# Chunked attention with a gated convolution on one Trainium2 core: a new order of the same pieces, new buffer homes, and a new division of small work between engines

## The chip, the cores and the metric

The kernel runs on one core of a Trainium2 chip (trn2). The metric is the device time of one execution in microseconds (us); the kernel before has three timed runs and one profiled execution. "ns" marks nanoseconds. The engines are TensorE (PE in the rows; PEld are its weight loads), VectorE (DVE), ScalarE (ACT), GpSimd (POOL) and SyncE (SP), whose queue issues the loads and stores.

## What is computed

Inputs q, k, v are float32 of shape (8, 8, 576, 64): batch, heads, sequence, head size. Attention runs inside chunks of 64 positions; its output, with the heads side by side, is x of shape (8, 576, 512):

```python
scores = np.matmul(q_c, k_c.transpose(0, 1, 2, 4, 3)) / 8
attn = np.exp(scores - np.max(scores, axis=-1, keepdims=True))
attn = attn / (np.sum(attn, axis=-1, keepdims=True) + 1e-09)
x = np.matmul(attn, v_c)
gate = 1.0 / (1.0 + np.exp(-sum(conv_w[j] * xp[:, j:j + S, :] for j in range(5))))
out = (gate * (x @ w_val)) @ w_out
```

xp is x with four rows of zeros ahead of each batch (a causal convolution of five taps per column). w_val and w_out are 512 x 512.

## The kernel before, in words

The 4608 rows of x are cut into 9 groups g of 512. A group has two head pairs p and, for the matrix products, four column blocks of 128 (m, c, hp) and four row blocks t. All work is cut into small pieces, and one long string, ORDER (line 18), lists 1157 of them; a loop (line 516) reads the string and calls a function for each, and every engine does its own pieces in the order of the list. Nothing reorders them: a late piece holds up all that stands behind it on its engine. A second table, SLOTS (line 95), says which of a few fixed buffers each tile takes, in order of creation. A piece that writes a buffer waits until the readers of what it held are done. The large matrix products work on float32 split in two rounded parts (high and low), three matmuls for each product.

The pieces, with their engine where no letter is added (D at the end of a name puts a piece on VectorE, G on GpSimd):

- Loads on SyncE: lq, lk, lv (g, p), 512 KB each, into six buffers ld0 to ld5; lw n c, a 512 KB block of w_val (n = v) or w_out (n = o), into one of four acc buffers; lc, the taps. st g t stores 256 KB.
- Weights: w1 to w7, wb, w9 turn a loaded block into its high and low parts (VectorE, ScalarE, GpSimd).
- TensorE: W n, n warm-up matmuls on zeros, whose result nobody reads; S g p b, 32 score matmuls of 64 x 64 (two halves b in one two-bank score buffer); sp, four matmuls that subtract a row maximum; T g p, eight transposes; A g p, 64 matmuls of attention times v, into two of four banks ps; V g m c, three matmuls of 128 x 512 of x @ w_val (lines 448 to 454), four pieces c to a bank; P g t c, three matmuls of the last product (lines 477 to 483).
- Softmax: mx (row maxima, VectorE), sb (subtract, VectorE, reads the score buffer and so frees it), ex and ep (exponential, ScalarE), ea (another form, 16 exponentials with sums, ScalarE), sm (sums and reciprocals, VectorE), ng and rc (small, VectorE), nm (divide, GpSimd), ec (transposed scores out of their banks, ScalarE).
- x: xr (high part) and xc (copy) on ScalarE, xd (low part) on VectorE, each on a half u; all three read the bank. hl fills the halo (GpSimd).
- Convolution: k0 (first tap, ScalarE), k g hp j (taps 1 to 4, VectorE, one multiply-and-add of 128 x 516 each), sg (sigmoid, ScalarE; exponential and sigmoid need different tables, and a change loads one).
- Gate: vc (x @ w_val out of its bank, ScalarE), gs (times the gate, VectorE) or gm (both in one, VectorE), gr (high part, ScalarE), gd (low part, GpSimd). oc copies a finished output block (ScalarE).

```python
    def pr(g, t, c):
        ...
        for n, (y, w) in enumerate(((gh, wh), (gh, wl), (gl, wh))):
            run(E.matmul, o_ps[g, t], lhsT=y[g, c][:, ts], rhs=w["o"][:, c, :], start=(c == 0 and n == 0),
                stop=(c == NH - 1 and n == 2))
```

So P g t c needs gr g c and gd g c, and, for c = 0 or the first of a bank's four, the bank; V g m c needs xr and xd of both halves.

Of the kernel before, what the change touches and what calls it, by code (L numbers as in the profile page):

```python
# [21 lines left out]
lv 1 0,sb 1 0,xc 0 0 1,xr 0 0 1,wb v 0,T 0 1,xd 0 0 0,ex 1 0,xd 0 0 1,S 1 1 0,w1G v 3,ec 0 1,S 1 1 1,sm 1 0,w7G v 1,
V 0 3 0,lq 2 1,w5 v 3,lw o 0,w2 v 3,mx 1 1,A 0 1,lk 2 1,nm 1 0,xc 0 0 0,lw o 1,lw o 3,V 0 2 0,sb 1 1,xr 0 1 0,lk 3 0,
w6 v 1,T 1 0,xr 0 1 1,w3 v 3,wbD v 1,xc 0 1 0,S 2 0 0,xc 0 1 1,w4 v 3,S 2 0 1,w6 v 2,xd 0 1 0,w7G v 3,ec 1 0,V 0 3 1,
lq 4 0,xd 0 1 1,lq 3 0,V 0 2 1,w3 c 0,w1 c 0,wb v 2,mx 2 0,w6 v 3,A 1 0,w5 c 0,w2 c 0,ex 1 1,w4 c 0,wb v 3,sb 2 0,
V 0 2 2,lv 1 1,w5 o 0,V 0 3 2,xr 1 0 0,w3 o 0,w9,V 0 2 3,sm 1 1,ex 2 0,k0G 0 1,V 0 3 3,hl 1,vc 0 2,w1G o 0,S 2 1 0,
# [10 lines left out]
V 2 1 0,w4 o 1,sg 0 1,V 2 0 3,k 1 2 1,w6 o 3,k0 2 0,V 2 1 1,gdD 0 0,vc 2 0,w7 o 1,V 2 3 2,gr 0 3,k 1 0 2,V 2 1 2,
k0 1 1,k 1 2 2,V 2 2 0,gr 0 2,gdD 0 3,w6 o 1,V 2 1 3,w3 o 2,w2 o 2,ng 4 0,P 0 1 0,gs 0 1,vc 2 1,k 1 2 3,V 2 2 1,gr 0 1,
wbD o 1,V 2 3 3,gdD 0 1,V 2 2 2,w4 o 2,ex 3 1,P 0 2 0,k 1 3 1,V 2 2 3,vc 2 3,w7 o 2,T 3 0,gdD 0 2,w6 o 2,sm 3 1,vc 2 2,
P 0 1 1,wb o 2,ea 4 0,P 0 3 0,wbD o 3,P 0 0 0,k 1 1 1,P 0 0 1,nmD 3 1,P 0 1 2,P 0 1 3,k 1 3 2,P 0 0 2,k 1 1 2,P 0 0 3,  # L40
ec 3 0,k 1 0 3,P 0 2 1,k 1 1 3,oc 0 1,P 0 3 1,k 1 0 4,k0 2 1,P 0 2 2,oc 0 0,k0D 2 2,k 1 1 4,T 3 1,k 2 2 1,P 0 3 2,
k 1 3 3,sg 1 0,A 3 0,k 1 2 4,ec 3 1,rc 4 0,P 0 2 3,sg 1 1,k 1 3 4,lk 5 0,xr 3 0 0,P 0 3 3,k 2 1 1,hl 3,oc 0 2,k 2 0 1,
S 4 1 0,nm 4 0,oc 0 3,S 4 1 1,xd 3 0 0,xr 3 0 1,A 3 1,lq 5 1,xd 3 0 1,xc 3 0 0,lk 5 1,mx 4 1,xc 3 0 1,V 3 3 0,lk 7 1,
gsG 1 0,xr 3 1 0,V 3 2 0,k0 2 3,xd 3 1 0,V 3 2 1,xr 3 1 1,gsG 1 1,xc 3 1 0,xd 3 1 1,V 3 3 1,gr 1 0,k 2 2 2,V 3 1 0,
sg 1 2,gd 1 0,sb 4 1,V 3 3 2,xc 3 1 1,V 3 2 2,k 2 3 1,V 3 0 0,k 2 1 2,V 3 0 1,k 2 3 2,ex 4 1,V 3 2 3,k 2 2 3,V 3 1 1,
k 2 3 3,vc 3 2,V 3 0 2,k 2 1 3,V 3 3 3,k 2 1 4,sg 1 3,P 1 0 0,k 2 3 4,gr 1 1,V 3 1 2,k 2 0 2,V 3 1 3,gdD 1 1,k 2 0 3,
T 4 0,vc 3 1,k 2 2 4,P 1 0 1,gs 1 2,sg 2 2,V 3 0 3,k 2 0 4,ec 4 0,gsG 2 2,P 1 1 0,sm 4 1,gr 1 2,S 5 0 0,vc 3 3,S 5 0 1,
hl 4,sg 2 1,gdD 1 2,nm 4 1,P 1 1 1,lv 7 1,vc 3 0,mx 5 0,st 0 2,P 1 3 0,gr 2 2,lq 6 0,sg 2 3,P 1 3 1,sb 5 0,sg 2 0,
P 1 2 0,k0 3 1,gs 2 0,P 1 0 2,k0 3 3,gs 1 3,S 5 1 0,k 3 1 1,gr 1 3,S 5 1 1,k0 3 2,gdD 2 2,P 1 1 2,gd 1 3,lv 4 0,st 0 1,
gr 2 0,mx 5 1,P 1 2 1,lk 6 1,P 1 3 2,k 3 1 2,gd 2 0,P 1 2 2,sb 5 1,ex 5 0,P 1 0 3,k0 3 0,gs 2 1,P 1 3 3,gs 2 3,gr 2 1,  # L50
P 1 1 3,sm 5 0,gd 2 1,P 1 2 3,oc 1 1,oc 1 0,S 6 0 0,k 3 1 3,oc 1 2,S 6 0 1,st 1 0,ex 5 1,A 4 0,k 3 3 1,lv 4 1,lk 8 1,
# [5 lines left out]
V 4 3 3,hl 5,sg 3 1,gsG 3 2,V 4 2 0,oc 2 3,V 4 1 0,vc 4 3,gs 3 1,nm 5 0,gr 3 2,V 4 1 1,sm 6 0,sg 3 0,A 5 1,k 4 1 3,
V 4 2 1,nm 6 0,xr 5 1 0,lv 5 0,st 0 0,xr 5 1 1,T 5 0,xd 5 1 0,sg 3 3,sb 6 1,V 4 2 2,xc 5 1 0,xc 5 1 1,V 4 2 3,gsG 3 3,
ec 5 0,xd 5 1 1,S 7 0 0,S 7 0 1,gs 3 0,gr 3 1,A 5 0,k 4 3 1,vc 4 2,lq 7 1,gr 3 0,k0D 5 2,V 4 0 0,mx 7 0,xr 5 0 0,
gd 3 0,xc 5 0 1,V 4 1 2,xc 5 0 0,k0D 5 3,V 4 0 1,k 4 1 4,k0 5 1,V 4 1 3,k 4 3 2,gr 3 3,V 4 0 2,xr 5 0 1,xd 5 0 0,  # L60
gd 3 3,V 4 0 3,xd 5 0 1,P 3 3 0,gdD 3 1,gd 3 2,vc 4 0,vc 4 1,P 3 2 0,k0 5 0,P 3 3 1,k 4 3 3,sg 4 1,V 5 0 0,k0 4 2,
# [5 lines left out]
xd 6 0 1,S 7 1 0,S 7 1 1,gs 4 1,A 6 1,lv 7 0,k 5 0 4,st 3 1,mx 7 1,lq 8 0,T 7 0,xc 6 1 1,lv 8 1,xc 6 0 1,st 3 0,
V 5 2 2,k 5 3 4,xr 6 1 0,V 5 1 0,gs 4 3,xr 6 1 1,xd 6 1 0,V 5 2 3,sg 5 3,xcD 6 1 0,sg 4 0,V 5 1 1,k 5 1 4,gr 4 1,
k0G 6 3,V 6 1 0,vc 5 2,xd 6 1 1,V 6 1 1,sb 7 1,gsG 4 0,V 6 0 0,V 6 2 0,gdD 4 1,k0G 6 2,V 6 2 1,k0D 6 0,gsG 5 3,V 6 2 2,
ex 7 1,V 6 1 2,gr 4 3,k 6 2 1,gsG 4 2,V 6 1 3,gr 4 0,ecD 7 0,V 6 2 3,k0 6 1,V 6 0 1,k 5 2 4,gr 4 2,V 6 0 2,sm 7 1,  # L70
vc 6 1,hl 7,gd 4 0,V 5 1 2,vcD 6 2,S 8 1 0,nm 7 1,sg 5 2,S 8 1 1,A 7 0,sg 5 1,lk 8 0,st 2 3,gdD 4 2,lv 8 0,V 6 0 3,
# [500 lines left out]
```

## Time and profile before

| | us |
|---|---|
| median of 3 timed runs | 285.98 (285.41 to 287.75) |
| span of the profiled execution, first to last instruction | 286.4 |
| TensorE busy | 274.4 (96%) |
| VectorE busy | 245.8 (86%) |
| ScalarE busy | 198.1 (69%) |
| GpSimd busy | 105.2 (37%) |

Times in rows count from the first instruction. Every instruction of the list comes from one helper, so all rows carry line 160; they are told apart by tile names (buffer numbers left out: ps for ps3; t is t2 and t4 with a digit, t2i one buffer of t2). A "busy" TensorE includes matmuls that overlap: a 128 x 512 matmul lasts about 400 ns, but the next starts 0.23 us after it.

### The profile page before, as it was taken

What the parts mean: (1) busy time and instruction counts of PE and PEld (TensorE: products, weight loads), DVE (VectorE), ACT (ScalarE), POOL (GpSimd) and SP (SyncE); (2) the same over time, 40 slices, a digit from 0 to 9 for tenths busy, and PEclk for the clock granted to TensorE, in tenths of its full rate; (3) what the DMA queues carried; (4) which work ended last, traced back from release to release, by engine and by line L of the source; (5) the groups of instructions that cost most, each with busy time, mean ns of one, the idle gap of its engine ahead of it and who ended that gap; (6) DMA issues with size and microseconds to landing.
All of it is one profiled execution on the core that took longest, in us unless ns stands there. A gap on an engine that the chain in (4) does not pass through costs nothing.

```text
span 286.4 us, 7971 instructions
## 1 busy us (share of the span) xinstructions
PE 274.4 (96%) x3344; PEld 217.3 (76%) x3347; DVE 245.8 (86%) x357; ACT 198.1 (69%) x451; POOL 105.2 (37%) x93
## 2 busy tenths in 40 slices
...
GB/s 280 416 391 359 380 239 130 169 181 260 3 2 78 222 0 185 221 223 211 86 185 2 73 201 218 173 144 44 39 0 1 39 89 61 0 100 49 110 171 195
DMA packets 14291, 42.47 MB, mean 148 GB/s; under 512 B 1712, under 2 KB 1712, under 8 KB 14256
## 3 DMA queue, kind: packets, MB, share of 16 engines
...
## 4 chain that ended last, share of the span: by engine, by line
PE 69%; DVE 19%; DMA 3%; issue 3%; POOL 2%; ACT 2%; SPq 0%; POOLq 0%
PE ps L160 61%; DVE acc L160 8%; PE s L160 5%; DVE t L160 4%; PE et L160 4%; DVE rs L160 3%; DMA ld<-in_v 2%; DMA ld<-in_q 1%; POOL acc L160 1%; POOL t L160 1%; DVE mx L160 1%; ACT x L160 1%; DVE t2o L160 1%; DVE t4a L160 0%; DVE x L160 0%
## 5 line engine op out<-in xcount | busy, mean ns | idle before, releaser
L160 DVE SCALAR_TENSOR_TENSOR acc<-x,cw,acc 128x516 f32<-128x516 f32 (+1 forms) x144 | 105.1, 771 | 0.9 <-POOL acc L160 0.6
L160 PE MATMUL ps<-t,v_hi 128*128 128x512 f32 x240 | 85.3, 402 | 0.0
L160 PE MATMUL ps<-t,v_lo 128*128 128x512 f32 x136 | 53.9, 396 | 0.0
L160 PEld LDWEIGHTS ps<-t,v_hi 128*128 128x128 f32 x240 | 45.2, 188 | 11.0 <-issue 0.5
L160 PE MATMUL ps<-o_hi,t 128*128 128x512 f32 x120 | 46.4, 403 | 0.8 <-ACT x L160 0.7
L160 PE MATMUL ps<-o_lo,t 128*128 128x512 f32 x76 | 30.0, 395 | 0.0
L160 DVE TENSOR_REDUCE mx<-s 128x16 f32<-128x1024 f32 x18 | 21.8, 1211 | 9.3 <-PE s L160 9.2
L160 PEld LDWEIGHTS ps<-t,v_lo 128*128 128x128 f32 x136 | 25.7, 189 | 5.1
L160 PEld LDWEIGHTS ps<-o_hi,t 128*128 128x128 f32 x120 | 22.5, 188 | 7.3 <-ACT x L160 1.1
L160 POOL TENSOR_TENSOR t<-e_row,rs 128x1024 f32<-128x1024 f32 x13 | 26.4, 2033 | 4.2 <-DVE rs L160 3.4
L160 PEld LDWEIGHTS s<-ld,ld 64*64 64x64 f32 x1152 | 19.4, 139 | 9.6 <-issue 7.7
L160 ACT CAST t<-ps 128x512 fp32r<-128x512 f32 x34 | 19.4, 596 | 10.0 <-PE ps L160 8.1
L160 PE MATMUL s<-ld,ld 64*64 64x64 f32 x1152 | 22.0, 227 | 2.9 <-issue 1.9
L160 ACT ACTIVATE e_row<-s,mx 128x64 f32<-128x64 f32 x64 | 19.0, 352 | 4.7 <-DVE mx L160 4.7
L160 POOL COPY x<-x 128x16 f32<-128x16 f32 x8 | 2.8, 354 | 52.6 <-DVE acc L160 44.9
L160 PEld LDWEIGHTS ps<-t,ld 64*64 64x64 f32 x960 | 16.3, 140 | 5.0 <-issue 2.1
L160 PE MATMUL ps<-t,ld 64*64 64x64 f32 x960 | 18.1, 225 | 1.9 <-DVE t2i L160 1.1
L160 POOL TENSOR_SCALAR acc<-x,cw 128x516 f32<-128x516 f32 (+1 forms) x7 | 12.7, 1820 | 19.2 <-ACT x L160 7.4
L160 ACT ACTIVATE acc<-x,cw 128x516 f32<-128x516 f32 (+1 forms) x24 | 17.6, 740 | 1.9 <-DVE x L160 1.8
L160 ACT ACT_TABLE_LOAD x14 | 18.0, 1283 | 0.9 <-PEq L561 0.7
L160 DVE TENSOR_REDUCE rs<-e_row 128x16 f32<-128x1040 f32 x14 | 17.2, 1228 | 1.6 <-ACT e_row L160 1.6
L160 ACT COPY x<-ps 128x512 f32<-128x512 f32 (+3 forms) x38 | 16.0, 476 | 3.3 <-issue 2.0
...
## 6 DMA issues: line engine op xcount, KB each, us to landing
...
```

Of the source, the lines that this page charges most:

```text
L160: return tc.keep_in_program_order(fn(*args, **kwargs))
```

## The change

The list ORDER is written anew: the same 1157 pieces for the same work, in another order on all engines. SLOTS is new for nearly all buffers. The warm-up matmuls go from 31 (W 8, 15, 6, 2) to 17 (W 10, 4, 1, 2). Some pieces change engine. By kind, before to after: first taps k0 on ScalarE 24 to 20, VectorE 5 to 3, GpSimd 7 to 13; gd on VectorE 21 to 17, GpSimd 15 to 19; gs on VectorE 18 to 17, GpSimd 14 to 15; nm on GpSimd 14 to 13, VectorE 4 to 5; xc on VectorE 9 to 4, ScalarE 27 to 32; oc on VectorE 11 to 10; vc on VectorE 3 to 4; ec on VectorE 2 to 3; w7 on VectorE 2 to 5, GpSimd 6 to 3; w1 on VectorE 1 to 2; wb on VectorE 4 to 3. The rest of the code changes only so that halves of x may come in either order:

```diff
-ORDER = """zw,lk 0 0,zi,lq 0 0,W 8,lw v 2,lw v 0,lq 0 1,zr 1,zm,lk 0 1,lw v 1,zr 0,lv 0 0,lq 1 0,S 0 0 0,S 0 0 1,W 15,mx 0 0,
+ORDER = """zw,zi,zr 0,zr 1,lk 0 0,lq 0 0,W 10,zm,lw v 2,w1 v 2,w3 v 2,w2G v 2,S 0 0 0,S 0 0 1,mx 0 0,sb 0 0,lw v 0,w5 v 0,w5 v 2,
...
-    mx="021021021021021021",
+    mx="001111122000000111",
...
+    def x_of(g):
+        if g not in xs:
+            xs[g] = tile_of("x", [P, NH, XW], F32)
+        return xs[g]
+
     def hl(g, on=G):
 
-        xs[g] = x = tile_of("x", [P, NH, XW], F32)
+        x = x_of(g)
...
     def xr(g, p, u):
-        if u == 0:
+        if (g, p) not in xh:
             xh[g, p] = tile_of("xh", [P, 2, T], F32R)
...
     def xd(g, p, u):
-        if u == 0:
+        if (g, p) not in xl:
             xl[g, p] = tile_of("xl", [P, 2, T], F32R)
```

The first pair of fences is SyncE's list at the start, its 8th to 17th entries before and its 8th to 19th after (ld, acc: the buffers; in_q, in_k, in_v, in_moe_w_val, in_moe_w_out: the inputs). Before:

```order
L160 DMA ld2_102<-in_v 128x1024
L160 DMA ld1_104<-in_q 128x1024
L160 DMA ld5_157<-in_k 128x1024
L160 DMA ld0_161<-in_k 128x1024
L160 DMA acc1_166<-in_moe_w_val 128x1024
L160 DMA ld4_226<-in_q 128x1024
L160 DMA ld3_230<-in_q 128x1024
L160 DMA ld1_334<-in_v 128x1024
L160 DMA ld5_341<-in_k 128x1024
L160 DMA raw_cw_343<-in_moe_conv_w 128x40
```

After:

```order
L160 DMA acc3_193<-in_moe_w_out 128x1024
L160 DMA acc0_210<-in_moe_w_val 128x1024
L160 DMA ld4_234<-in_k 128x1024
L160 DMA ld5_243<-in_q 128x1024
L160 DMA ld0_247<-in_k 128x1024
L160 DMA ld1_289<-in_v 128x1024
L160 DMA ld2_332<-in_q 128x1024
L160 DMA ld3_404<-in_q 128x1024
L160 DMA ld0_406<-in_v 128x1024
L160 DMA ld5_443<-in_v 128x1024
L160 DMA raw_cw_446<-in_moe_conv_w 128x40
L160 DMA ld1_473<-in_q 128x1024
```

The v of group 0 (lv 0 0) was the 8th load and is now the 13th, behind two weight blocks and the q and k of group 1; the 20th entry after, not shown, is lk 2 0.

The second pair is TensorE's list around S 2 0, the scores of group 2 (s: score buffer; et: transpose banks; ps: V banks; t42, t43 and so on: high and low part of x). Before:

```order
L160 MATMUL et0_476<-ident_61,t49_459 128x128 x8
L160 MATMUL s0_490<-ld5_341,ld3_230 64x64 x32
L160 MATMUL ps2_410<-t42_348,v_hi_66 128x512
L160 MATMUL ps2_410<-t42_348,v_lo_68 128x512
L160 MATMUL ps2_410<-t4a_365,v_hi_66 128x512
```

After:

```order
L160 MATMUL ps0_458<-t42_326,v_hi_66 128x512
L160 MATMUL ps0_458<-t42_326,v_lo_68 128x512
L160 MATMUL ps0_458<-t43_340,v_hi_66 128x512
L160 MATMUL s0_482<-ld2_480,ld1_473 64x64 x32
L160 MATMUL et0_517<-ident_61,t48_515 128x128 x8
```

The piece V 0 3 1 (three rows on ps) now stands ahead of the scores of group 2, and the transposes T 1 0 behind them.

The third pair is SyncE's list around the v of group 2, second pair (lv 2 1). Before:

```order
L160 DMA ld2_823<-in_v 128x1024
L160 DMA acc2_825<-in_moe_w_out 128x1024
L160 DMA ld0_1007<-in_v 128x1024
L160 DMA ld5_1015<-in_k 128x1024
L160 DMA ld4_1029<-in_k 128x1024
```

After:

```order
L160 DMA ld0_853<-in_q 128x1024
L160 DMA ld4_897<-in_v 128x1024
L160 DMA ld4_997<-in_v 128x1024
L160 DMA ld0_1006<-in_k 128x1024
L160 DMA ld2_1096<-in_k 128x1024
```

Before, lv 2 1 (ld0_1007) takes the buffer of lq 3 1, which S 3 1 reads; now (ld4_997) it takes that of lv 2 0 (ld4_897), which A 2 0 reads. On TensorE, A 2 0, T 2 1, two V pieces and S 4 0 stood between S 3 1 and A 2 1; now S 3 1, T 2 1 and seven V pieces stand between A 2 0 and A 2 1.

## Rows read from the trace of the kernel before

**Rows 1.** The page: busy us, share of the span, instructions of each engine.

```profile
PE 274.4 (96%) x3344; PEld 217.3 (76%) x3347; DVE 245.8 (86%) x357; ACT 198.1 (69%) x451; POOL 105.2 (37%) x93
```

**Rows 2.** Stretches: length, then busy PE, PEld, DVE, ACT, POOL; clock, DMA share, GB/s.

```profile
10.00:20.00 10.00, 9.09 (x219) 5.98 (x220) 9.11 (x15) 6.24 (x10) 4.06 (x4) 1.00 1.03 410
20.00:30.00 10.00, 7.34 (x189) 5.45 (x192) 9.41 (x15) 9.47 (x16) 7.87 (x7) 1.00 0.99 362
30.00:40.00 10.00, 10.00 (x191) 7.87 (x184) 6.96 (x10) 6.23 (x13) 8.25 (x9) 0.83 0.79 287
...
60.00:70.00 10.00, 9.17 (x184) 7.63 (x177) 9.28 (x13) 9.10 (x20) 7.18 (x6) 1.00 0.87 298
...
180.00:190.00 10.00, 8.99 (x100) 7.10 (x98) 9.33 (x11) 6.59 (x10) 9.25 (x9) 1.00 0.25 95
190.00:200.00 10.00, 9.81 (x216) 8.01 (x219) 9.82 (x13) 9.28 (x18) 6.11 (x5) 1.00 0.38 131
200.00:210.00 10.00, 9.33 (x60) 7.33 (x51) 9.97 (x16) 5.01 (x16) 3.96 (x3) 1.00 0.08 28
```

**Rows 3.** The chain that ended last: start us, us, what.

```profile
27.82 1.94 issue
...
59.46 5.08 DMA ld<-in_v
...
220.13 62.66 PE ps L160 x386
```

**Rows 4.** Stretches around the first hole, columns as in rows 2.

```profile
27.00:30.00 3.00, 1.06 (x41) 0.75 (x43) 2.58 (x6) 2.82 (x5) 1.80 (x2) 1.00 1.02 385
...
31.00:34.50 3.50, 3.50 (x66) 2.61 (x68) 3.50 (x6) 0.87 (x2) 1.75 (x2) 0.51 1.01 359
```

**Rows 5.** Timeline of PE, 118 to 123 us: start us, us, instruction, count.

```profile
118.98 0.40 PE L160 MATMUL ps<-o_hi,t2o 128*128 128x512 f32 x1
119.31 1.16 PE L160 MATMUL s<-ld,ld 64*64 64x64 f32 x64
...
121.33 0.49 PE L160 MATMUL ps<-o_hi,t2q 128*128 128x512 f32 x1
121.67 0.39 PE L160 MATMUL ps<-o_lo,t2q 128*128 128x512 f32 x1
121.89 0.40 PE L160 MATMUL ps<-o_hi,t 128*128 128x512 f32 x1
```

**Rows 6.** Timeline of DVE and POOL, three places where both work in SBUF.

```profile
128.90 2.87 DVE L160 SCALAR_TENSOR_TENSOR acc<-x,cw,acc 128x516 f32<-128x516 f32 x4
128.11 1.71 POOL L160 TENSOR_SCALAR acc<-x,cw 128x516 f32<-128x516 f32 x1 [2.02 <-issue]
139.78 1.80 DVE L160 TENSOR_TENSOR t<-t,t2n 128x512 f32<-128x512 f32 x1 [0.42 <-ACT t2n L160]
139.75 1.29 POOL L160 TENSOR_TENSOR t2p<-t2c,t2d 128x512 f32<-128x512 f32 x1
189.92 2.13 DVE L160 TENSOR_TENSOR t2o<-t,t2n 128x512 fp32r<-128x512 f32 x1
```

**Rows 7.** Groups of instructions: count, busy us, mean ns of one, idle before.

```profile
L160 DVE SCALAR_TENSOR_TENSOR acc<-x,cw,acc 128x516 f32<-128x516 f32 (+1 forms) x144 | 105.1, 771 | 0.9 <-POOL acc L160 0.6
L160 DVE TENSOR_REDUCE mx<-s 128x16 f32<-128x1024 f32 x18 | 21.8, 1211 | 9.3 <-PE s L160 9.2
L160 POOL TENSOR_SCALAR acc<-x,cw 128x516 f32<-128x516 f32 (+1 forms) x7 | 12.7, 1820 | 19.2 <-ACT x L160 7.4 <-DVE x L160 5.1 <-ACT t2n L160 2.9
L160 ACT ACT_TABLE_LOAD x14 | 18.0, 1283 | 0.9 <-PEq L561 0.7
```

**Rows 8.** Timeline of the first loads' users: start us, us, instruction, idle before.

```profile
5.47 1.99 PE L160 MATMUL s<-ld,ld 64*64 64x64 f32 x64 [0.71 <-DMA ld<-in_q]
7.18 0.63 POOL L160 TENSOR_SCALAR t<-acc 128x512 f32<-128x512 f32 x1 [5.79 <-DMA acc<-in_moe_w_val]
```

**Rows 9.** Waits of PE: who waited for whom, us in total, times, longest.

```profile
PE ps L160 <- DVE t2i L160: 1.1, 1, 1.1
```

More of the change, by code (lines that the diff above doesn't have):

```diff
@@ L22 @@
[L22 to L26, printed above, removed]
@@ L37 @@
[L37 to L41, printed above, removed]
@@ L42 @@
[L42 to L51, printed above, removed]
@@ L57 @@
[L57 to L61, printed above, removed]
@@ L67 @@
[L67 to L71, printed above, removed]
@@ new lines @@
+xc 2 1 0,S 4 0 0,S 4 0 1,V 2 3 0,V 2 3 1,xd 2 1 0,gr 0 3,k0 1 2,V 2 2 0,V 2 2 1,mx 4 0,k 1 2 1,ng 4 0,xc 2 1 1,gr 0 1,
+gdD 0 1,V 2 3 2,V 2 1 0,w7 o 2,w4 o 1,k 1 0 3,V 2 3 3,w5 o 1,w7 o 1,hl 2,k 1 2 2,k 1 3 1,ex 3 1,T 3 0,k0 2 2,k 1 2 3,
+w6 o 2,gr 0 0,k0 1 1,V 2 2 2,w6 o 3,gdD 0 0,V 2 0 0,V 2 0 1,V 2 1 1,V 2 0 2,V 2 0 3,k 1 3 2,ec 3 0,gr 0 2,vc 2 3,w6 o 1,
+vc 2 0,V 2 1 2,V 2 1 3,vc 2 1,sm 3 1,gdD 0 2,k0 2 0,k0 2 3,wbD o 2,k 1 1 1,wbD o 3,P 0 1 0,V 2 2 3,k 1 2 4,gdD 0 3,
+P 0 0 0,lk 6 0,wb o 1,P 0 0 1,vc 2 2,P 0 0 2,P 0 1 1,nmD 3 1,lv 3 0,P 0 1 2,P 0 1 3,k 1 3 3,ea 4 0,k 1 1 2,k 2 0 1,
@@ new lines @@
+k 3 1 3,A 4 0,oc 1 1,gdD 2 1,sm 5 1,nmD 5 1,xr 4 0 1,xd 4 0 1,gr 2 0,gdD 2 0,S 6 0 0,S 6 0 1,k0G 3 2,xc 4 0 0,mx 6 0,
+k 3 2 1,T 4 1,gd 2 3,k 3 3 1,gr 2 2,gd 2 2,xr 4 0 0,k 3 2 2,lv 4 1,P 2 2 0,P 2 2 1,P 2 2 2,P 2 2 3,ec 4 1,xd 4 0 0,
+ex 5 0,k 3 3 2,k 3 3 3,xc 4 0 1,oc 2 2,P 2 1 0,P 2 1 1,k 3 0 1,k 3 0 2,lq 6 1,P 2 1 2,P 2 1 3,oc 2 1,sm 5 0,nm 5 0,
+A 4 1,xc 4 1 0,xr 4 1 1,lk 7 0,T 5 1,xr 4 1 0,xc 4 1 1,k0G 4 3,k0G 4 2,ec 5 1,P 2 3 0,P 2 0 0,P 2 0 1,xd 4 1 0,sb 6 0,
+P 2 3 1,ex 6 0,k 3 0 3,k 3 3 4,k 3 2 3,k 3 2 4,P 2 3 2,P 2 3 3,k0G 4 1,P 2 0 2,P 2 0 3,oc 2 0,st 2 0,k 3 0 4,oc 2 3,
```

132 lines of the change are left out of this document (76 added, 56 removed).

## The prediction, made before the changed kernel ran

> **What bounds the kernel now.** I read four views: the busy shares, the same by stretches, the chain of waits, and single instructions by name where the chain changes hands. TensorE is busy 274.4 of 286.4 us and VectorE 245.8 [rows 1]. By stretches [rows 2] there are three parts. Until about 35 us TensorE has holes (7.34 of 10 us from 20 to 30) and VectorE too (6.96 from 30 to 40). Then both run almost without a pause, TensorE with 0.83 us missing at 60 to 70 and 1.01 and 0.67 us at 180 to 190 and 200 to 210. The chain shows the last 62.66 us before the final copy and store as one stretch of TensorE [rows 3], so the end is the time at which TensorE reaches it, and that is its work plus what it lost before.
>
> What was lost early has two pieces. At 27.82 us TensorE stands for 1.94 us in the middle of the scores of group 2; the profile names no releaser ("issue") [rows 3]. It had been busy for 1.06 of those 3 us, and from 31 to 34.5 us its granted clock is 0.51, the 1.2 GHz level [rows 4]. That costs 3.5 x 0.49 = 1.7 us.
>
> In the middle the two engines are locked together. A matmul waits for a difference, a released bank or a scaled row that VectorE makes, and its date is set by the VectorE work that stands ahead in the list. I count both queues up to a place. On TensorE a V or P piece is 0.70 us (three matmuls, 0.23 apart, 121.67 to 121.89 [rows 5]), half a score piece 0.55, a transpose piece 0.87, an A piece 1.03. A VectorE instruction takes its group's mean less the 0.06 by which neighbours overlap (four k in 2.87 us, 0.72 each [rows 6]; means in [rows 7]). Before S 5 1 0 stand 88 V or P, 22 half scores, 9 T, 8 A and the four row-maximum matmuls: 90.7 us. VectorE's queue up to sb 5 0, which frees the bank, holds 146 instructions (48 k, 11 mx, 8 sb, 8 sm, 16 xd, the rest small): 99.7 us. I call 9.0 us the lead that this place asks. The tightest such places before lie at 9 to 9.6 us from 70 us to 165 us, about 8 after that.
>
> **The change, part by part.**
>
> Start. The loads come at 410 GB/s [rows 2], so 512 KB take 1.28 us; the third has landed by 7.18, where GpSimd starts on it [rows 8]. In the new list lk 1 0 is the 12th load, so about 7.1 + 9 x 1.28 = 18.6 us, lv 0 0 the 13th, 19.9, lv 0 1 the 16th, 23.7, lk 2 0 the 19th large one, 27.6 (the first pair of fences in the section on the change). I follow the chain, each step with the mean of its group: S 0 1 waits for the sixth load, about 11.0, and takes 2.0 us, as S 0 0 did at 5.47 behind slow warm-up matmuls and a hole [rows 8]; S 1 0 ends 19.8, A 0 0 21.0, mx 1 0 and sb 1 0 22.3, ex 1 0 23.9, ec 0 1 24.9, A 0 1 25.9; sm 1 0, w4 v 3, mx 1 1, sb 1 1 on VectorE end 29.0 and free the score bank; S 2 0 ends 30.1. Before, S 2 0 ended at 30.57, with T 1 0 done and V 0 3 1 not; now the reverse, 0.87 against 0.70 us. So TensorE stands 0.3 us better there, and its holes are spread: none from 27 us on is over 0.6 us. I expect no fall of the clock after it, 1.7 us, though no row shows how it behaves in the new pattern. Bounds: with a wait like the unnamed one and the low clock again, -0.3 + 1.9 = +1.6; with the chain faster by 1.6 as well, -3.6. I take -2.0, what the chain gives. The 14 warm-up matmuls that go cost nothing by themselves: what follows them waits for a load or for VectorE. VectorE has no hole from 30 to 40 in this chain; it had 3.0 us, so it runs 3.0 us earlier.
>
> The load lv 2 1. Before, it went out at 59.46, when S 3 1 was done, and took 5.08 us, with only A 2 0, T 2 1, two V and S 4 0 (4.4 us) ahead of its use; TensorE stood 0.8 us [rows 2, 3]. Now it waits for A 2 0, and S 3 1, T 2 1 and seven V, 6.9 us, stand between. 5.08 fits: -0.8. It fails from a landing of 6.9 us on; if the queue holds it back so long, 0.
>
> Late waits. 1.01 + 0.19 + 0.67 = 1.9 us of holes from 180 to 210 [rows 2]; the longest, 1.1, is A 7 0 on a bank that VectorE copies out (vcD 6 2, into t2i) [rows 9]. There the old list asks a lead of 166.1 us of TensorE work against 174.2 of VectorE, 8.1, and 8.0 at P 5 0 0 (189.2 against 197.2). The new list asks 5.9 at V 7 0 2 (177.1 against 183.0) and 2.4 at V 8 1 2 (209.6 against 212.0). With 2 to 5 us of slack these go: -1.9, bounds -1.9 and 0.
>
> Changes of shape. Between V or P and 64-wide pieces TensorE loses 0.1 us going in (118.98 to 119.31) and 0.1 coming out (121.33 to 121.67) against 0.23 [rows 5]. Such visits fall from 20 to 18, 0.4 us; T pieces right after V or P fall from 12 to 5, each with the 0.1 on the way out, 0.7 us. Where VectorE sets the pace it is worth nothing, so I take half: -0.5, bounds -1.1 and 0.
>
> The pace in the first half. Here the new list asks more. At V 3 1 0: 64 V or P, 22 half scores, 9 T, 8 A, 73.9 us, against 127 VectorE instructions, 84.5: 10.6. At P 2 2 0: 96, 26, 10, 9, 100.4 us, against 163 instructions up to gdD 2 0 (51 k, 12 mx, 9 sb, 9 sm, 17 xd, 6 gd, 6 gs), 112.0: 11.6. Against the 9.6 that TensorE met before, that is 2.0 more. VectorE is 3.0 us earlier and TensorE 2.0 + 0.8 = 2.8; the difference, 0.2, pays part, and TensorE must wait 1.8. Bounds: 0 (gdD 2 0 could meet a free VectorE) and +3 (VectorE not earlier). I take +1.8.
>
> Loads of the other engines. VectorE's pieces change by -2 first taps, -5 xc, -4 gd, -1 gs, -1 oc, +1 vc, +1 nm, +1 ec, +3 w7, +1 w1, -1 wb, about -4 us; that is in the leads above. ScalarE: -1.2 us of copies and taps, but 16 table loads instead of 14, +2.6 [rows 7]; it is 69% busy [rows 1], so 0, and at most +1. GpSimd takes on six first taps (1.82 each), four gd, one gs, one wb and gives up one nm, three w7, a w1: +12 us on 105. It waits for others two thirds of the time, but it slows VectorE when both read SBUF: at 139.78 a VectorE product of two SBUF tiles took 1.80 us beside a GpSimd one of 1.29, and at 189.92 one took 2.13 [rows 6]; six such long ones from 139 to 200 us, 6.6 us in all, on 105 us of GpSimd. Pro rata +0.8, but no long one before 139 us, where VectorE sets the pace in the new list: +0.2, bounds 0 and +7.
>
> The Trainium skill (SBUF — State Buffer, on the two separate sides) says that a VectorE instruction with two SBUF inputs and a GpSimd one that reads SBUF exclude each other for the whole instruction. At 139.78 the trace agrees. Beside the first tap at 128.11 (1.71 us) it does not: four k with two SBUF inputs ran in 2.87 us, unstretched [rows 6]. By the rule the added 12 us would block VectorE where it holds such work; the second rival below gives what that costs as a mechanism of this kernel.
>
> **Sum.** -2.0 - 0.8 - 1.9 - 0.5 + 1.8 + 0.2 = -3.2 us on the profiled execution: 286.4 to 283.2. What lies behind the last matmul (one copy, one store, 3.6 us) stays [rows 3]: 286.4 - 220.13 - 62.66. The span is 0.4 us above the median 285.98, so 282.8 as a median, 1.1% less. About 1%, 2.9 us, is what a measurement of this kernel can tell from no change.
>
> **Rivals.**
>
> First: the start does not hold. The unnamed wait of 1.94 us comes at another score piece, or the clock falls after the new hole at 23 to 25 us (1.5 us in this chain). For it: the loads stay at 400 GB/s and the new list has the same burst of small matmuls there; against it: the holes are more evenly spread. Start 0 instead of -2.0; VectorE is then no earlier either, so the pace still costs 1.2 (2.0 less the 0.8 of lv 2 1): 285.98 - 0.8 - 1.9 - 0.5 + 1.2 + 0.2 = 284.2; with half of a second such wait 285.2, which I take.
>
> Second, slower: GpSimd holds up VectorE. Each of the six added first taps, four gd and the gs falls between two-input instructions of VectorE and costs the 1.1 us of 139.78: 11 x 1.1 = 12 us, of which the seven before 130 us, where the lead is tight, count whole: +7.7 instead of +0.2. That gives 290.3; from four of them before 130 us on (4.4 us) it outweighs the gains. For it: 139.78 and 189.92; against it: 128.11, and no long one in the first 139 us. With five of the seven, 5.5 us, it is 288.1.
>
> Third: no pace is paid and the start is 1.6 us better still: 282.8 - 1.8 - 1.6 = 279.4. For it: VectorE is 4 us lighter; against: the wait on banks stays a chain through two engines.
>
> Fourth: the list moves much but the lead at P 2 2 0 keeps TensorE at its old date, and the late holes only move: 286.0.
>
> **How the numbers follow.** Forecast 0.50, its own range 281.0 to 284.2, two thirds of it below 283.1, the mark of 1%. First rival 0.18 (no change). Second 0.15 (slower). Third 0.09 (faster). Fourth 0.08, of which 0.02 on the slow side. Faster by over 1%: 0.33 + 0.09 = 0.42. Slower: 0.15 + 0.02 = 0.17. Within 1%: 0.17 + 0.18 + 0.06 = 0.41. The range for 8 in 10 leaves out half of the second rival and most of the third: 280.0 to 288.0.
>
> **What would show it.** Right: no stretch with a granted clock below 1 from 27 to 40 us; VectorE above 9.5 of 10 us from 30 to 40; TensorE's row on in_v gone; no hole over 0.5 us from 180 to 210; small holes at V 3 1 0 and P 2 2 0, 1 to 2 us in all, on VectorE. Wrong: an unnamed wait again before 40 us; k, gs or gd of 1.6 us and more before 130 us; a wait of TensorE on ScalarE longer than 1 us; a chain that after 220 us still runs through VectorE.

## The result, and the profile after

The changed kernel takes 289.91 us (289.79 to 290.64), the kernel before 285.70 in the same comparison: ratio 1.0142, interval 1.0096 to 1.0189. It is slower, by 4.2 us, where 282.8 was forecast. Executions of one kernel scatter by 2 us and more, so the sections below give medians and the ratio to the kernel before with its interval. The ratio leaves out executions of more than 1.5% above the fastest of their kernel, which a median keeps (three of ten at f4_before_cold), so it is not always the quotient of two medians.

The page after, busy times and the granted clock in 40 slices (7.2 us each):

```profile
PE 273.1 (95%) x3333; PEld 218.3 (76%) x3333; DVE 251.6 (87%) x350; ACT 200.5 (69%) x453; POOL 118.3 (41%) x100
PEclk9676999999999999999999999999999999999999
```

The clock is low from the second slice to the fourth. The stretches of [rows 2] and two shorter ones, same columns:

```profile
10.00:20.00 10.00, 6.44 (x80) 4.32 (x80) 9.47 (x17) 6.81 (x11) 4.59 (x6) 0.67 1.02 411
20.00:30.00 10.00, 9.61 (x270) 7.95 (x270) 6.93 (x10) 5.38 (x9) 6.39 (x6) 0.67 0.69 248
30.00:40.00 10.00, 9.41 (x222) 7.49 (x221) 9.86 (x14) 8.83 (x17) 6.77 (x5) 1.00 0.84 307
...
60.00:70.00 10.00, 8.98 (x159) 7.29 (x158) 9.96 (x14) 9.72 (x20) 8.02 (x6) 1.00 0.59 206
180.00:190.00 10.00, 10.00 (x47) 8.10 (x46) 9.78 (x15) 8.71 (x15) 2.42 (x2) 1.00 0.36 143
190.00:200.00 10.00, 10.00 (x167) 8.15 (x165) 9.68 (x14) 8.19 (x16) 3.76 (x3) 1.00 0.59 182
200.00:210.00 10.00, 10.00 (x163) 8.31 (x163) 9.89 (x16) 7.10 (x15) 4.06 (x5) 1.00 0.02 7
...
9.40:16.20 6.80, 5.01 (x71) 3.23 (x72) 6.34 (x11) 3.92 (x7) 3.25 (x4) 0.51 1.02 411
19.70:26.50 6.80, 6.24 (x136) 5.09 (x137) 3.89 (x6) 2.94 (x7) 5.74 (x6) 0.50 0.78 282
```

Two things stand here. The late holes are gone, as forecast (10.00 of 10 from 180 to 210). And TensorE runs at the 1.2 GHz level for 13.6 of the first 26.5 us (in this execution; another one, x1_after below, has half of that). "Busy" hides that: 9.61 of 10 from 20 to 30 us looks full, but 6.5 of it runs at half speed.

What TensorE waited for (who for whom, us in total, times, longest), and the chain at the start (start, us, what):

```profile
PE s L160 <- DMA ld<-in_q: 4.3, 1, 4.3
PE s L160 <- DMA ld<-in_k: 2.5, 1, 2.5
PE ps L160 <- DMA ld<-in_v: 1.6, 2, 0.9
...
PE s L160 <- issue: 1.0, 1, 1.0
```

```profile
2.08 6.40 DMA acc<-in_moe_w_val
...
11.13 8.89 DMA ld<-in_k
...
20.16 1.99 PE s L160 x64
...
32.60 1.16 PE s L160 x64
```

SyncE stands at lw v 3, whose buffer ScalarE still reads, until 9.74 us; lk 1 0 goes out at 11.13 and has landed at 20.02. In between the loads' queue is full: its share is 1.02 from 9.4 to 16.2 us, and the eighth load lands at 13.53. S 1 0 then takes 1.99 us instead of 1.16, and S 2 0 (the 32.60 row) ends at 33.76.

### The profile page after: what moved, and what is told of

Read it like the earlier page. It is cut to its first block, busy times and chain, and to the rows that moved or that the text cites. A ratio compares the mean times of both kernels' runs of the same rounds, so it can differ in the third digit from the quotient of the medians.

```text
span 288.8 us, 7943 instructions
## 1 busy us (share of the span) xinstructions
PE 273.1 (95%) x3333; PEld 218.3 (76%) x3333; DVE 251.6 (87%) x350; ACT 200.5 (69%) x453; POOL 118.3 (41%) x100
## 4 chain that ended last, share of the span: by engine, by line
PE 46%; DVE 24%; DMA 9%; ACT 8%; issue 8%; POOL 1%; SPq 1%; POOLq 1%; DVEq 0%; ACTq 0%
PE ps L160 39%; DVE acc L160 11%; DVE t L160 4%; DMA ld<-in_v 4%; PE s L160 4%; PE et L160 3%; DMA ld<-in_k 3%; ACT t L160 3%; DMA acc<-in_moe_w_val 2%; DVE rs L160 2%; ACT e_row L160 2%; DVE mx L160 2%; DVE e_row L160 1%; SPq L160 1%; POOL t L160 1%
## 5 line engine op out<-in xcount | busy, mean ns | idle before, releaser
L160 DVE SCALAR_TENSOR_TENSOR acc<-x,cw,acc 128x516 f32<-128x516 f32 (+1 forms) x144 | 113.8, 819 | 4.4 <-POOL acc L160 3.4
L160 PE MATMUL ps<-t,v_lo 128*128 128x512 f32 x112 | 44.3, 395 | 0.0
L160 PE MATMUL ps<-o_hi,t 128*128 128x512 f32 x84 | 30.5, 398 | 0.1
L160 PEld LDWEIGHTS ps<-t,v_lo 128*128 128x128 f32 x112 | 21.1, 188 | 4.4
L160 POOL TENSOR_SCALAR acc<-x,cw 128x516 f32<-128x516 f32 (+1 forms) x13 | 22.1, 1706 | 2.2 <-DVE x L160 1.8
L160 DVE TENSOR_TENSOR t<-ps,t 128x512 fp32r<-128x512 f32 (+1 forms) x26 | 17.5, 683 | 4.9 <-ACT t L160 4.8
L160 ACT ACTIVATE t<-acc 128x512 f32<-128x512 f32 (+8 forms) x28 | 12.8, 494 | 10.5 <-DMA acc<-in_moe_w_val 7.0
L160 PEld LDWEIGHTS ps<-o_hi,t 128*128 128x128 f32 x84 | 15.8, 188 | 4.0 <-POOL t L160 0.5
L160 PE MATMUL et<-ident,t 128*128 128x128 f32 x136 | 18.8, 282 | 0.0
L160 PE MATMUL ps<-t,ld 64*64 64x64 f32 x832 | 16.2, 228 | 2.3 <-DMA ld<-in_v 1.6
L160 ACT CAST t<-ps 128x512 fp32r<-128x512 f32 x28 | 15.8, 598 | 3.6 <-PE ps L160 3.6
```

The costliest lines, as they stand in the source:

```text
L160: return tc.keep_in_program_order(fn(*args, **kwargs))
```

## The experiments

Where loads or warm-ups move, SLOTS follows the new order (not shown).

**The kernel before, a second profile.** No edit.

> The kernel before, unchanged, profiled a second time. Theory A: the execution on which the prediction was built was not a typical one; its unnamed wait of 1.94 us at 27.82 and the half clock from 31 to 34.5 us cost about 2 us that the median does not have. Then this profile has no wait over 0.5 us in the scores of group 2, a clock of 1 from 27 to 40 us, and a span of about 284. Rival: the wait and the half clock belong to the kernel; the span is again 286.4 and the time 286.

285.73 us, ratio 1.0018 (0.9983 to 1.0053). This profile's span is 283.9 and its execution took 285.64, so 1.8 us lie outside the span, as they do after the change (288.8 and 290.64). Stretch and TensorE's timeline at the place of [rows 4]:

```profile
31.00:34.50 3.50, 3.50 (x75) 3.02 (x75) 3.47 (x6) 2.33 (x4) 1.80 (x2) 1.00 1.02 405
```

```profile
26.88 0.58 PE L160 MATMUL s<-ld,ld 64*64 64x64 f32 x24
28.53 0.81 PE L160 MATMUL s<-ld,ld 64*64 64x64 f32 x40 [1.07 <-issue]
```

Half of theory A holds: no half clock, and 2.5 us less span. The unnamed wait is there again, at the same 24th matmul of S 2 0, but 1.07 us long instead of 1.94. The execution I had predicted from was one of the long ones. Against this profile S 2 0 ends 4.4 us later after the change (29.34 to 33.76), and the whole span is 4.9 us longer: nearly all of the loss is made before 34 us.

**The first loads, one way.**

```diff
 lw v 1
+lq 1 0
+lk 1 0
 lw o 3
 lw v 3
 lk 1 1
-lq 1 0
-lk 1 0
 lv 0 0
```

> The changed kernel with lq 1 0 and lk 1 0 issued right after lw v 1, ahead of lw o 3, lw v 3 and lk 1 1 (the ld buffers renamed to fit). Theory A, the start is what makes the changed kernel slower: S 1 0 starts at about 17.6 instead of 20.16 us and the time falls by 2 to 2.6 us, from 289.9 to about 287.5. Rival, the loss is made later, by VectorE beside GpSimd and the tighter lead: S 1 0 comes earlier all the same, but by 130 us TensorE is as late as before the edit, and the time stays within 0.5 us of 289.9.

290.98 us, ratio 1.0178 (1.0108 to 1.0247): no gain at all. S 1 0 starts at 17.95, close to what theory A said. But lw v 3 now lands at 18.19, w3 v 3 stands waiting for it on VectorE, the chain goes on through w7G v 1 on GpSimd, and T 0 1 waits for nm 0 1 behind it:

```profile
PE s L160 <- DMA ld<-in_q: 5.5, 2, 5.1
...
PE et L160 <- POOL t L160: 2.4, 1, 2.4
```

The edit traded one late load for another. It doesn't decide between the theories.

**More warm-ups.**

```diff
-S 0 0 0,S 0 0 1,mx 0 0,
+S 0 0 0,S 0 0 1,W 16,mx 0 0,
...
-T 0 0,ec 0 0,
+T 0 0,W 9,ec 0 0,
```

> The changed kernel with two more warm-up pieces, 16 matmuls behind S 0 0 and 9 behind T 0 0, in the two holes where TensorE waits for loads. If the low clock (0.5 from 9.4 to 16.2 and from 19.7 to 26.5 us) comes of these holes and costs time: no clock below 1 after 12 us, S 1 0 takes 1.16 instead of 1.99 us, A 0 0 and T 0 1 gain 1.5 us together, and the time falls by 1.5 to 2.3 us to about 288. Rival, the low clock is covered by the waits for loads and by VectorE's chain: within 0.5 us of 289.9.

288.36 us, ratio 1.0103 (1.0064 to 1.0143): 1.6 us better by the medians, 1.1 by the ratios, whose intervals overlap. The mean granted clock is 1.0 (0.976 in the profile above). S 1 0 takes 1.16 us, and then a wait stands in the open that the profile above doesn't have. Timeline of TensorE, VectorE and GpSimd:

```profile
19.66 1.16 PE L159 MATMUL s<-ld,ld 64*64 64x64 f32 x64 [1.07 <-DMA ld<-in_k]
...
69.75 0.74 PE L159 MATMUL ps<-t,v_hi 128*128 128x512 f32 x2 [1.11 <-DVE t L159]
...
66.80 2.30 DVE L159 SCALAR_TENSOR_TENSOR acc<-x,cw,acc 128x516 f32<-128x516 f32 x1
...
66.62 1.92 POOL L159 TENSOR_TENSOR t<-e_row,rs 128x1024 f32<-128x1024 f32 x1
```

k 1 0 2 starts 0.18 us after nm 3 0 and ends 0.56 after it: it stood until nm 3 0 was done. xd 2 1 0 behind it is late, and TensorE with it.

**Loads and warm-ups.** The load order of e1_loads, and:

```diff
-S 0 0 0,S 0 0 1,mx 0 0,
+S 0 0 0,S 0 0 1,W 16,mx 0 0,
```

> The changed kernel with the earlier loads lq 1 0 and lk 1 0 and the 16 warm-up matmuls behind S 0 0. Theory A: both gains add, 3.5 to 4.5 us, to about 286. Rival, they pay for the same hole, or the middle takes them back: 287.5 to 290.

289.73 us, ratio 1.0115 (1.0056 to 1.0173). Warm-ups gain 1.3 us on e1_loads by the medians, and T 0 1 still waits 2.4 us for GpSimd. The rival holds: the loads of this order pay nothing.

**The first loads, another way,** with W 16 and W 4:

```diff
 lw v 3
-lk 1 1
-lq 1 0
 lk 1 0
+lq 1 0
 lv 0 0
+lk 1 1
 lq 1 1
-lq 2 1
+lk 2 0
 lv 0 1
 lv 1 1
 lc
 lq 2 0
-lk 2 0
+lq 2 1
```

> The changed kernel with warm-ups (16 behind S 0 0, 4 behind T 0 0) and another order of the first loads, in which lw v 3 keeps its place: lk 1 0, lq 1 0, lv 0 0 ahead of lk 1 1 and lq 1 1, and lk 2 0 in the place of lq 2 1. The warm-ups alone gave 288.4. Theory A, what is left of the loss at the start is two loads (lk 1 0 landing at 19.5 where TensorE waits 1.1 us for it, lk 2 0 landing at 30.8 where it waits 1.0): both waits go, S 2 0 starts at 29 to 29.5 instead of 31.0, and the time falls by 1.3 to 2 us to about 286.7. Rival, VectorE's and GpSimd's list sets the date of S 2 0: it starts at 30.5 or later, and the time stays within 0.5 us of 288.4.

288.43 us, ratio 1.0077 (1.0043 to 1.0112). As a time this is the rival. The profile is of one of its longer executions (290.67): S 2 0 starts at 30.18, between what the two foresaw, and of what that gains unnamed waits take 2.5 us in three places (1.5 of it at 96 us, ahead of S 5 0, of which more at h3_warm_k_inv).

**The VectorE instruction beside GpSimd,** with W 16 and W 9:

```diff
 xd 2 1 1
-k 1 0 2
 xd 2 1 0
 mx 4 0
+k 1 0 2
 k 1 2 1
```

> The changed kernel with the two warm-up pieces (16 and 9) and one VectorE instruction moved: k 1 0 2 behind mx 4 0 instead of ahead of xd 2 1 0, so that it no longer lies beside nm 3 0 on GpSimd. With the warm-ups alone k 1 0 2 took 2.30 us there (mean of its kind 0.8) and TensorE waited 1.1 us for xd 2 1 0. Theory B, GpSimd reading SBUF holds up VectorE at the one place where TensorE waits for it: k 1 0 2 takes 0.75 us, the wait at 68 us goes, and the time falls by 1.0 to 1.4 us from 288.4 to about 287.2. Rival, another wait takes its place at once (a load, a later difference): within 0.4 us of 288.4.

286.57 us, ratio 0.9995 (0.9965 to 1.0026): theory B, 1.8 us better than e2_warm (1.3 in the table of two by two below), no longer distinguishable from the kernel before.

**Loads of v.** With W 16 and W 9; SyncE's list:

```diff
-st 1 2
-st 0 0
 lv 5 0
+st 1 2
+st 0 0
 lq 7 0
-lv 8 0
+lv 6 1
...
-lv 6 1
+lv 8 0
```

> The changed kernel with the two warm-up pieces and loads of v earlier: lv 6 1 and lv 8 0 change places (and buffers) in SyncE's list, and st 1 2 and st 0 0 go behind lv 5 0. With the warm-ups alone TensorE waits 0.7 us for lv 5 0 at 145 us and 0.7 for lv 6 1 at 175. Theory C: both waits go and the time falls by 1 to 1.4 us from 288.4 to about 287.2. Rival: TensorE then meets the VectorE results that it now reaches earlier, and the gain is below 0.4 us.

288.66 us, ratio 1.0067 (1.0038 to 1.0096): no gain. The wait for lv 5 0 went, and S 7 0, next on TensorE, waits as long for lq 7 0, which stands behind the two stores again (0.74 us at 148.5). Neither theory had looked at the next load in the queue.

**Fewer warm-ups in the kernel before.**

```diff
-S 0 0 0,S 0 0 1,W 15,mx 0 0,
+S 0 0 0,S 0 0 1,W 4,mx 0 0,
...
-S 0 1 1,W 6,lq 1 1,
+S 0 1 1,W 1,lq 1 1,
```

> The kernel before with the changed kernel's number of warm-ups at the same places: W 15 becomes W 4 and W 6 becomes W 1. If the few warm-ups by themselves lower the clock: stretches at 0.5 before 27 us as in the changed kernel, and 1 to 2 us more than 285.7. Rival, the changed kernel loses its clock by its late loads alone: clock 1 and 285.7 within 0.5 us.

289.49 us (285.48 to 291.13), ratio 1.0053 (1.0007 to 1.0100): by the ratio 1.5 us. The profiled execution is a long one, 289.77. Stretch and TensorE's timeline:

```profile
9.00:19.00 10.00, 6.40 (x98) 5.01 (x101) 8.38 (x13) 5.44 (x10) 3.76 (x4) 0.66 1.03 413
```

```profile
61.52 1.18 PE L160 MATMUL ps<-t,ld 64*64 64x64 f32 x47
65.36 0.50 PE L160 MATMUL ps<-t,ld 64*64 64x64 f32 x17 [2.66 <-issue]
```

The clock falls in the old list too, from 12.1 to 18.9 us, so for the first fall few warm-ups are enough and the new loads are not needed; the second fall of the profile after (19.7 us) has no counterpart here. At S 2 0 that costs 1.3 us (28.15 against 26.88). The rest of this execution's loss comes at a place I had not foreseen: an unnamed wait of 2.66 us inside A 2 1, which no profile of the kernel before has.

**All edits together.** e2_warm's idea with W 16 and W 4, the loads of f1_start and f3_inv, k 1 0 2 moved, and on GpSimd:

```diff
-w1G v 3
 nm 0 1
+w1G v 3
```

> The changed kernel with all edits that the theories ask for: warm-ups (16 and 4), k 1 0 2 behind mx 4 0, the first loads in the order of f1_start, lv 6 1 for lv 8 0, two stores behind lv 5 0, and w1G v 3 behind nm 0 1 on GpSimd. Warm-ups and k alone gave 286.6. Theory: what is left of the start (about 1 us in the quiet executions of f1_start) and of the waits for v (0.7 and 0.3) comes off too: 284.5 to 285.3, below the kernel before at about 286. Rival: TensorE reaches the tight places of the middle (V 3 1 0, P 2 2 0) earlier than VectorE allows and waits there: 286 to 286.6, with holes of 0.5 us and more between 95 and 130 us.

286.28 us, ratio 1.0010 (0.9979 to 1.0042). The rival's number, but not its sign: there is no hole of 0.5 us from 95 to 130 us. S 7 0 waits at 147 us for lq 7 0, as in f3_inv, 1.04 us, and S 5 0 waits 1.1 us at 94, of which more at h3_warm_k_inv. The profiled execution was the longest of twelve (288.55).

**The move alone.** The edit of f2_k without warm-ups:

```diff
-k 1 0 2
 xd 2 1 0
 mx 4 0
+k 1 0 2
```

> The changed kernel with k 1 0 2 behind mx 4 0 and nothing else. If the price of the collision adds to that of the clock: 289.9 less 1.3 to 1.8, about 288.3. Rival: with the late start VectorE is ahead of TensorE at that place and the collision is covered: 289.9 within 0.5 us.

290.09 us (287.75 to 293.43, four executions), ratio 1.0106 (1.0040 to 1.0171): the rival, as far as four executions with so wide a scatter show it.

**Warm-ups, move and loads of v.** f2_k, and of f3_inv:

```diff
-st 1 2
-st 0 0
 lv 5 0
+st 1 2
+st 0 0
...
-lv 8 0
+lv 6 1
```

> The changed kernel with warm-ups (16 and 9), k 1 0 2 moved, and the loads of v of f3_inv; beside f2_k this is the loads of v alone. If these waits are lost time: 0.5 to 1 us below 286.6, 285.6 to 286.1. Rival, as f3_inv read: no gain, 286.6 within 0.4.

287.41 us, ratio 1.0054 (1.0021 to 1.0088). No gain, again lq 7 0 (1.22 us at 148). And a second meeting of VectorE and GpSimd. Timelines of this run:

```profile
88.62 3.08 DVE L160 SCALAR_TENSOR_TENSOR acc<-x,cw,acc 128x516 f32<-128x516 f32 x2
...
89.24 1.91 POOL L160 TENSOR_TENSOR t<-e_row,rs 128x1024 f32<-128x1024 f32 x1
```

and of z1_loads_late (below), the same instructions:

```profile
89.06 1.33 DVE L160 SCALAR_TENSOR_TENSOR acc<-x,cw,acc 128x516 f32<-128x516 f32 x2
...
89.69 2.47 POOL L160 TENSOR_TENSOR t<-e_row,rs 128x1024 f32<-128x1024 f32 x1
```

nm 4 0 starts once 0.62 and once 0.63 us behind the first of two k, where the first ends and the second begins. The recorded start of the second k lies 0.04 to 0.05 us ahead of that of nm 4 0 in both runs, so the starts do not tell which of the two got in first; who stood tells it. In the first run it is the second k, which stands 1.7 us, and with it mx 4 1 and sb 4 1 behind it and TensorE, whose S 5 0 needs the bank that sb 4 1 reads (1.48 us at 94.20, "issue" in the rows). In the second nm 4 0 stands 0.6 us, which costs nothing.

**The kernel before, with its longest late wait taken away.**

```diff
 ecD 7 0
+vcD 6 2
 k 5 2 4
 sm 7 1
-vcD 6 2
```

> The kernel before with one instruction moved on VectorE: vcD 6 2 ahead of k 5 2 4 and sm 7 1 instead of behind them. In its trace A 7 0 waits 1.1 us for it at 186 us, because four VectorE instructions beside GpSimd ones ahead of it took 3.9 us more than their mean. If TensorE's end is its work plus its holes: 0.8 to 1.3 us below the kernel before. Rival: mx 8 1, sb 8 1 and the waits at 191 and 200 us then end where they ended: within 0.4 us.

286.32 us, ratio 1.0005 (0.9975 to 1.0035). The rival: the row on t2i of [rows 9] is gone, and T 7 1 waits for nm 7 1 instead:

```profile
190.09 1.09 PE L160 MATMUL et<-ident,t 128*128 128x128 f32 x8 [1.13 <-POOL t L160]
```

**A table of two by two, on one chip.** The kernels of the changed one, of e2_warm, of h2_k_only and of f2_k again.

> The changed kernel, unchanged, as one corner of a table of two by two on one chip. 289.9.

> The changed kernel with the warm-ups of e2_warm. If the prices add: 1.5 us below x1_after, 288.4, with the clock at 0.99 and more instead of 0.98.

> The changed kernel with k 1 0 2 behind mx 4 0 alone. If the prices add: 1.3 to 1.8 us below x1_after, 288.1 to 288.6. If the late start covers the collision: within 0.5 us of x1_after.

> The changed kernel with both. If the prices add: 3.0 to 3.3 us below x1_after, 286.6 to 286.9. If f2_k was scatter: 288.4.

| | median us | ratio to before (286.13) |
|---|---|---|
| changed | 290.06 | 1.0111 (1.0051 to 1.0170) |
| with warm-ups | 288.86 | 1.0083 (1.0047 to 1.0118) |
| with k 1 0 2 moved | 289.28 | 1.0102 (1.0062 to 1.0142) |
| with both | 287.54 | 1.0023 (0.9988 to 1.0059) |

Both together give 2.5 us, somewhat less than expected; the move alone is not distinguishable from nothing by its ratio. One by one the two give 1.2 and 0.8 us by the medians, 0.8 and 0.3 by the ratios: with these intervals the times alone do not decide whether the prices add. The profile of x1_after shows what can hide the move. TensorE and VectorE, timeline:

```profile
64.47 0.89 PE L160 MATMUL s<-ld,ld 64*64 64x64 f32 x48
67.02 0.46 PE L160 MATMUL s<-ld,ld 64*64 64x64 f32 x16 [1.66 <-issue]
...
67.29 2.27 DVE L160 SCALAR_TENSOR_TENSOR acc<-x,cw,acc 128x516 f32<-128x516 f32 x1
```

An unnamed wait in S 4 0 holds TensorE for 1.66 us just before it would wait for VectorE. It covers the collision. With the warm-ups this wait is absent (e2_warm, x2_warm, x4_warm_k), and where the k is not moved the collision costs 1.1 us. So the changed kernel pays for one of the two; that only both edits together take the price away is read from these traces, and the times agree with it without showing it.

The start of x1_after differs from the profile after, though the kernel is the same. Stretches, and TensorE's timeline (S 1 0, A 0 0, the end of S 1 1, S 2 0):

```profile
10.80:17.60 6.80, 5.62 (x73) 3.93 (x75) 6.31 (x12) 3.68 (x7) 2.62 (x3) 0.50 1.00 392
19.70:26.50 6.80, 4.54 (x192) 4.16 (x195) 5.83 (x8) 5.35 (x10) 6.19 (x6) 1.00 0.91 334
```

```profile
20.37 1.16 PE L160 MATMUL s<-ld,ld 64*64 64x64 f32 x64 [1.88 <-DMA ld<-in_k]
21.96 1.16 PE L160 MATMUL ps<-t,ld 64*64 64x64 f32 x64 [0.43 <-PE s L160]
26.73 0.35 PE L160 MATMUL s<-ld,ld 64*64 64x64 f32 x9 [1.24 <-issue]
31.24 1.16 PE L160 MATMUL s<-ld,ld 64*64 64x64 f32 x64 [0.34 <-DMA ld<-in_k]
```

The clock falls once and is back before the wait for lk 1 0; S 1 0 and A 0 0 take 1.16 us. An unnamed wait of 1.24 us stands in S 1 1, which the profile after does not have. This execution took 289.38 us all the same.

In x4_warm_k the k lies behind nm 3 0 and the wait is gone; VectorE, then GpSimd:

```profile
68.53 1.22 DVE L160 TENSOR_REDUCE mx<-s 128x16 f32<-128x1024 f32 x1
69.66 1.41 DVE L160 SCALAR_TENSOR_TENSOR acc<-x,cw,acc 128x516 f32<-128x516 f32 x2
...
67.77 1.91 POOL L160 TENSOR_TENSOR t<-e_row,rs 128x1024 f32<-128x1024 f32 x1
```

**The rest: loads in the middle, then at the start.** z1_loads_late has, beside the edits of x4_warm_k:

```diff
 st 2 0
-st 2 3
-lk 7 1
-st 1 2
-st 0 0
 lv 5 0
 lq 7 0
-lv 8 0
+st 2 3
+lk 7 1
+st 1 2
+st 0 0
+lv 6 1
...
-lv 6 1
+lv 8 0
```

> x4_warm_k with the loads lv 5 0 and lq 7 0 ahead of st 2 3, lk 7 1, st 1 2 and st 0 0, and lv 6 1 in the place of lv 8 0. If the waits for loads at 145 and 175 us (0.7 and 0.3 to 0.7 us) are lost time: 0.8 to 1.3 us below x4_warm_k, beside the kernel before 0.9 to 1.2 us better than x4_warm_k stands (287.5 against 286.1). If VectorE's results set the date there: within 0.4 us of x4_warm_k.

y1_all has these, the loads of f1_start, w1G v 3 behind nm 0 1, and:

```diff
-T 0 0,W 9,ec 0 0,
+T 0 0,W 4,ec 0 0,
```

> z1_loads_late with the first loads in the order of f1_start, 4 warm-ups behind T 0 0 instead of 9, and w1G v 3 behind nm 0 1. If the rest of the loss is late loads: 0.5 to 1 us below z1_loads_late and below the kernel before, 285 to 285.7. If GpSimd and ScalarE set the date of S 2 0: no difference to z1_loads_late.

z1_loads_late takes 285.40 us, ratio 0.9988 (0.9956 to 1.0019), 2.1 us less than x4_warm_k by the medians; but f2_k, the same kernel as x4_warm_k, had 0.9995, so this step alone is not clear of the scatter. y1_all takes 284.74 us against 286.21, ratio 0.9936 (0.9909 to 0.9963): faster than both kernels. Its waits of TensorE, and a stretch in which two loads were late:

```profile
PE s L160 <- DMA ld<-in_q: 2.2, 2, 1.6
PE s L160 <- ACT mh L160: 1.6, 1, 1.6
PE s L160 <- issue: 1.4, 2, 0.8
PE ps L160 <- DVE warm L160: 1.2, 1, 1.2
```

```profile
60.00:70.00 10.00, 10.00 (x163) 8.13 (x162) 9.96 (x15) 9.75 (x19) 8.74 (x8) 1.00 0.70 237
140.00:150.00 10.00, 10.00 (x168) 8.30 (x167) 9.01 (x13) 8.56 (x17) 9.90 (x8) 1.00 0.96 316
```

No load of v in the middle and no VectorE row but the first warm-up is left, and behind 34 us TensorE has no hole over 0.1 us. So what f2_k and x4_warm_k still lost was for the most part late loads; w1G v 3 and the five warm-ups, which y1_all changes too, were not tried apart. What is left at the start is 1.4 us of unnamed waits, 2.2 for loads and 2.5 behind ScalarE.

## Why the prediction was wrong

**The base.** "The span is 0.4 us above the median" set one execution's span beside another's time. The time is the span and 1.8 us, so the profiled execution of 286.4 took about 288.2, 2.2 above the median. The unnamed wait and the half clock of which I booked the half clock as a gain of the new list ("I expect no fall of the clock after it, 1.7 us") belong to that execution; b1_before_again has no half clock and 0.9 us less wait. Some 2 us of the forecast's error is this.

**The start, -2.0.** This is the step that failed most. I had S 1 0 ending at 19.8, A 0 0 at 21.0, S 2 0 at 30.1. In the profile after they ended at 22.15, 24.78 and 33.76, in x1_after at 21.53, 23.12 and 32.40. Two terms were mis-sized.

The loads, which I dated at 1.28 us each from the head of the list. lk 1 0 landed at 20.02 (x1_after 20.23) and not at 18.6: the ninth load landed at 14.82 and the tenth at 17.47, 2.65 us later, with the queue full. Why is open. It is not SyncE's stand at lw v 3, since the eighth load was under way until 13.53; and the kernel before has the same gap (ninth 14.81, tenth 17.63), where I could have read it. Further on a load goes out only when its buffer is free: lv 0 1 went out at 22.20, when S 1 0 had read lk 1 0 out of the same buffer, and lk 2 0 at 28.22, behind S 1 1. It landed at 32.00 instead of 27.6; in x1_after it went out at 27.14, landed at 31.11, and S 2 0 waited for it.

The clock: "the 14 warm-up matmuls that go cost nothing by themselves" looked at what the next instruction waits for and not at the clock after the hole. In the profile after S 1 0 and A 0 0 each took 1.99 us instead of 1.16. f4_before_cold shows a fall with few warm-ups in the old list, and 1.3 us for it at S 2 0. [rows 4] had shown a fall after a hole, and I had used it only where it spoke for the change. The Trainium skill says that a half-speed clock is what the array falls back to and that activity lifts it (TensorE: Matmul & The Clock Gate, "What's actually happening"); the granted clock of 0.51 from 9.4 us on, in and behind a hole of 4.3 us, agrees. But the second fall is not what makes the changed kernel slow: of its ten executions the three with a mean clock of 0.976 to 0.979 took 289.79 to 291.02 us, the seven with 0.985 to 0.988 took 288.53 to 291.94. Putting warm-ups back gave 1.2 to 1.6 us in three pairs of medians. They lift the clock and they also move the unnamed waits; how much of the gain is owed to which these runs do not part.

**lv 2 1, -0.8.** Held: no wait there. But b1_before_again waits 0.6 us at the same place for ScalarE's x, so the load was not all that held A 2 1. And lv 5 0 and lv 6 1 became late (0.7 and 0.9 us, at 148 and 178, the row on in_v of 1.6 that was to go), a load behind stores and a load on the buffer of the piece before it. I had put this at nothing: I had checked the one load that was late before, not every load of the new list.

**Late waits, -1.9.** Held: no hole from 180 to 210, against 1.9 us in b1_before_again.

**Pace, +1.8.** Failed. Neither V 3 1 0 nor P 2 2 0 has a hole, also not in y1_all, where TensorE comes earliest. The "lead" counted from two lists is no wait by itself: it was taken against the lead that TensorE met before, and nothing showed that this one was the limit. VectorE above 9.5 of 10 from 30 to 40 held (9.86), but VectorE was not 3.0 us earlier by it: it stood from 20 to 30 instead (6.93 of 10, 9.41 before [rows 2]). That no clock below 1 would come from 27 to 40 us held to the letter: the falls came earlier.

**Collisions, +0.2.** The mechanism of the second rival was right, its place and size were not. I priced the work that was added to GpSimd. The one long k before 125 us (2.29 us at 68.94) lies beside nm 3 0, which was on GpSimd before as well: the new order put them side by side. It is one instruction and 1.1 us where nothing covers it, not seven. In the whole profile nine VectorE instructions stood 0.85 us and more, 9.4 us together, against six and 6.6 us before; eight of them lie behind 150 us, where TensorE's only hole is the wait for lv 6 1.

**Shapes, -0.5.** Not measured apart; the account that follows closes without it.

Against the second profile of before the account closes to 0.2 us: +4.4 at S 2 0, -0.6 at A 2 1, -1.9 for the late waits, +1.6 late loads of v, +0.4 at 56 us (A 2 0 behind vc 1 3, itself behind ea 3 0's sixteen exponentials on ScalarE), +1.0 the unnamed wait, together 4.9, measured 4.9 (left out: at S 2 0 the new list has V 0 3 1 behind it instead of T 1 0, 0.2 us less work done).

The first rival (the start doesn't hold) came nearest in its mechanism. Its price had been 2.0 us, because its own bound (+1.6) stopped at the pattern of the profile that it knew.
